# Query blocks outermost, with the rest of the layer run inside the next block's attention

## The chip, the cores and the metric

The kernel runs on one core of one Trainium2 chip. A core has five engines that run side by side and meet only through semaphores: TensorE (PE in the profile; its weight loads are listed as PEld) multiplies matrices, VectorE (DVE) and ScalarE (ACT) work on rows of 128 partitions and can read the accumulators, GpSimd (POOL) works between tiles of SBUF, and SyncE (SP) issues the DMAs of this kernel. Each engine takes its instructions in the order in which they were written. PSUM, where TensorE writes, has 8 banks; one bank holds a tile of 128 x 512 float32.

The metric is the time of one execution on the device, in microseconds (us). Lower is better.

## The reference

One transformer block with adaptive layer norm, on 2048 rows of 512 features, 32 heads of 16 features, a feed-forward width of 1792, all in float32:

```python
mod = (_silu(c) @ w_mod).reshape(c.shape[0], 6, 1, -1)
sa, ca, ga, sb, cb, gb = (mod[:, 0], mod[:, 1], mod[:, 2], mod[:, 3], mod[:, 4], mod[:, 5])
h = _layernorm(x, axis=-1) * (1 + ca) + sa
x = x + ga * _A_ref(h, A_wqkv, A_wo)          # softmax attention, 32 heads, then @ wo
h = _layernorm(x, axis=-1) * (1 + cb) + sb
x = x + gb * _B_ref(h, B_w1, B_b1, B_w2, B_b2)  # gelu(h @ w1 + b1) @ w2 + b2
```

The attention is full: every query meets all 2048 keys, `scores = q . k / 4`, then softmax, then the weighted sum of `v`. The gelu is the tanh approximation.

## The kernel before, in words

**Number format.** TensorE is fed values of a reduced format (`float32r`, FR in the code). To keep accuracy each operand is split into a high part (the value rounded to FR) and a low part (the rest), and a product is made of three matmuls: high x high, low x high, high x low (`mm3`, L288). Splitting costs one copy and one subtraction per tile. For the scores the three products lie in the rows of one contraction: 48 rows (3 x 16 features) for a head, and 50 where two rows carry the negative maximum of the query (its high and low part) against rows of ones, so that a score comes out with the maximum already subtracted.

**Tiling.** Rows are split into 4 query blocks of 512 (`NB`, `TB`), keys into 16 chunks of 128 (`NKC`), heads into 8 groups of 4 (`NG`). A unit `u` is one group with one query block, 32 units in all (`NU`); group is the outer loop: `g, qb = divmod(u, NB)`. A step `s` is one key chunk of one unit; there are 512. The four heads of a group lie in two pairs; the two heads of a pair sit in rows 0 to 63 and rows 64 to 127 of the array (`r0 = (j % 2) * 64`), so two matmuls on opposite row halves can run together.

**Stages, one after the other.**

1. Modulation rows, layer norm, transposes, projections. For each block `b` the loop at L431 projects the first quarter of the keys and queries and all of V; then the loop at L480 projects the other quarters for all blocks, with maxima work put between the matmuls (`fill`). Projected q, k, v go to DRAM and come back in the layout of the scores (`build_k`, `build_q`, `load_v`).
2. Attention, the loop at L729. Each step issues four scores (`exp_step`, L712, matmul L724) with the exponentials on ScalarE (L727), two maxima pairs for a unit further on (`next_max`, `max_pair`, L359: two matmuls at L369 into one tile of two banks, one reduction of 1024 columns per partition on VectorE at L371), and the four `p @ v` matmuls of the step before (`pv_step`, L538, matmul L545). The `v` tiles carry a column of ones, so that the sum of the exponentials comes with the product. `max_rows` (L373) ends a unit's maxima: a reduction, a TensorE transpose, a copy, a split on GpSimd, and three DMAs that bring the row maxima into rows 48 and 49 of the query tile.
3. Output projection of block 0 runs inside the last unit's steps (`hooks`, L694); the others, the second layer norm and the feed-forward follow from L756 on. For each of 4 x 14 chunks of the feed-forward width `load_f` and `split_f` (L568, L576) load and split both weight matrices' tiles, `ffn1` (L760) makes 12 matmuls, one Gelu on ScalarE and a split, and `ffn2` (L777) adds 12 matmuls into four banks that stay open for the block. The list `plan` puts the other blocks' output projection and layer norm at fixed places among the chunks.

**PSUM.** Maxima have two tiles of two banks (`ps_mx`), scores one tile of two banks and one of one bank, used in turn (`ps_e`; three scores are evacuated by one 1024-wide and one 512-wide activation), `p @ v` one bank. Seven banks serve the loop with 4 + 3, one is for `pv`.

**Queues.** The whole order is written out by hand (`tc.manual_schedule()`). All DMAs are issued from SP, in order; one that has to wait for its data holds those behind it. Waits are semaphores set where a tile is written, read or reused.

## Time and profile before

| | |
|---|---|
| median of 3 runs | 2246.9 us (2242.72 to 2248.88) |
| profiled execution, first to last instruction | 2241.2 us |
| mean granted TensorE clock | 0.988 |
| TensorE busy | 1876.3 us, 84% |
| VectorE busy | 1555.4 us, 69% |
| ScalarE busy | 1189.5 us, 53% |
| GpSimd busy | 251.2 us, 11% |
| DMA | 121.87 MB, mean 54 GB/s |

The profiled execution is one run under the hardware profiler; 2241.2 us is its span, and the runs' median lies 5.7 us above that. "Busy" for TensorE is not the same as working at full rate: matmuls are pipelined, the next starts before the last has drained, and the listed duration of one holds that drain. The rate is read from the distance between starts. In a row of the groups view, "x1024 | 1245.7, 1226 | 401.0 <-PE mx L369 398.3" means 1024 instructions, 1245.7 us busy in all, 1226 ns each in the mean, and 401.0 us in which the engine sat idle just before them, of which 398.3 ended when TensorE finished a matmul of line 369. In a row of the timeline the first number is the start in us from the start of the span, the second the length, "x2" the count of instructions merged, and the bracket the idle time before and what ended it. Names left and right of "<-" are the tile written and the tiles read. The clock column is the share of full TensorE clock that the throttle granted.

### The profile page before, as it was taken

The page shows a single profiled execution, that of the slowest core. Times are in us where ns is not written, and L with a number is a line of the kernel's source. Part 1 is how long each engine was busy: PE and PEld are TensorE (multiplying, and loading weights), DVE is VectorE, ACT ScalarE, POOL GpSimd, SP SyncE. Part 2 cuts the span into 40 slices and gives each one's busy share as a digit, 9 for nine tenths or more (in the row PEclk, how much of TensorE's full clock was granted, in tenths as well). Part 3 has the DMA queues.
Part 4 walks back from the last instruction along what each step waited for, and adds up shares of the span by engine and source line. Part 5 has one row for each costly group of instructions (what it writes and reads, how often), then busy time and mean ns, then how long its engine had stood idle before and what let it go on. Part 6 is the DMA issues. An engine that isn't in the chain of part 4 may idle for free.

```text
span 2241.2 us, 27287 instructions
## 1 busy us (share of the span) xinstructions
PE 1876.3 (84%) x10586; PEld 884.1 (39%) x10586; DVE 1555.4 (69%) x1563; ACT 1189.5 (53%) x1597; POOL 251.2 (11%) x250
## 2 busy tenths in 40 slices
PE   8889788787888787878877887888788889999999
PEld 6655322222222222222222222222222235778787
DVE  5245677777777777777777777777777845773653
ACT  2211466666666666666666666666666664221222
POOL 3100001000000000000000000000000102453553
PEclk9998899999999999999999999999999999999999
DMA  6642410030030003000300300030000124432331
GB/s 235 173 168 95 77 26 21 11 60 11 11 51 11 11 11 52 11 11 13 58 11 11 51 11 11 11 51 11 11 15 17 44 82 120 130 113 75 113 113 57
DMA packets 93325, 121.87 MB, mean 54 GB/s; under 512 B 13114, under 2 KB 52026, under 8 KB 91834
## 3 DMA queue, kind: packets, MB, share of 16 engines
q1 hardware_dynamic: 93196, 120.13, 20.4%
q8 instruction: 83, 1.36, 0.3%
q14 instruction: 46, 0.38, 0.1%
HBM read 88.42 MB, written 31.67 MB: 54 GB/s over the span
## 4 chain that ended last, share of the span: by engine, by line
PE 70%; ACT 21%; issue 4%; DVE 3%; POOL 1%; DMA 1%; SPq 0%; ACTq 0%; POOLq 0%; DVEq 0%
PE pv L545 22%; PE e L724 21%; ACT p L727 20%; PE e L294 12%; PE mx L369 6%; PE mx L790 4%; PE e L649 2%; PE pv L790 1%; ACT osb L531 1%; DVE mxp L371 1%; PE mx L724 0%; DVE parts L305 0%; POOL w2l L583 0%; DMA rb<-rden 0%; DVE xin L263 0%
## 5 line engine op out<-in xcount | busy, mean ns | idle before, releaser
L371 DVE TENSOR_REDUCE mxp<-mx 128x2 f32<-128x1024 f32 x1024 | 1245.7, 1226 | 401.0 <-PE mx L369 398.3
L727 ACT ACTIVATE p<-e 128x1024 f32<-128x1024 f32 (+1 forms) x1323 | 1005.7, 809 | 548.5 <-PE e L724 544.1
L724 PE MATMUL e<-qst,kst 50*128 50x512 f32 x1984 | 633.6, 481 | 313.3 <-ACT p L727 306.8
L724 PEld LDWEIGHTS e<-qst,kst 50*128 50x128 f32 x1984 | 249.9, 184 | 939.4 <-ACT p L727 778.7
L545 PE MATMUL pv<-p,vg 128*32 128x512 f32 x4096 | 548.9, 607 | 0.0
L369 PE MATMUL mx<-kst,qst 48*128 48x512 f32 x2048 | 528.5, 417 | 0.0
L369 PEld LDWEIGHTS mx<-kst,qst 48*128 48x128 f32 x2048 | 233.4, 187 | 16.7 <-issue 12.3
L384 POOL CAST m<-mr 16x128 fp32r<-16x128 f32 x32 | 9.0, 280 | 1464.3 <-DVE mr L382 1464.3
L768 ACT ACTIVATE g<-e,b_c 128x512 f32<-128x512 f32 x56 | 38.6, 689 | 248.0 <-PE e L294 248.0
L545 PEld LDWEIGHTS pv<-p,vg 128*32 128x32 f32 x4096 | 80.9, 108 | 188.6 <-issue 183.1
L772 DVE TENSOR_TENSOR glo<-g,ghi 128x512 fp32r<-128x512 f32 x56 | 57.6, 1028 | 105.8 <-ACT ghi L771 105.7
L294 PE MATMUL e<-hThi,w 128*128 128x512 f32 x256 | 76.8, 447 | 22.6 <-DVE parts L305 19.3
L581 POOL TENSOR_TENSOR w1l<-w1r,w1h 128x512 fp32r<-128x512 f32 x56 | 76.8, 1371 | 164.5 <-DVE w1h L580 144.9
L304 ACT ACTIVATE parts<-e 128x512 fp32r<-128x512 f32 x32 | 19.1, 597 | 127.1 <-PE e L294 124.7
L583 POOL TENSOR_TENSOR w2l<-w2r,w2h 128x512 fp32r<-128x512 f32 x56 | 79.4, 1417 | 6.9 <-DVE w2h L582 6.5
L294 PE MATMUL e<-p,w1h 128*128 128x512 f32 x224 | 75.5, 398 | 3.8 <-ACT h L251 2.2
L790 PE MATMUL mx<-w2h,glo 128*128 128x512 f32 x168 | 66.1, 393 | 3.0 <-DVE glo L772 3.0
L294 PEld LDWEIGHTS e<-hThi,w 128*128 128x128 f32 x256 | 52.2, 213 | 40.7 <-DVE parts L305 22.2
L790 PE MATMUL mx<-w2h,ghi 128*128 128x512 f32 x168 | 65.6, 390 | 0.0
L790 PE MATMUL mx<-w2l,ghi 128*128 128x512 f32 x168 | 65.5, 390 | 0.0
L305 DVE TENSOR_TENSOR parts<-e,parts 128x512 fp32r<-128x512 f32 x32 | 21.8, 683 | 44.0 <-ACT parts L304 44.0
L582 DVE CAST w2h<-w2r 128x512 fp32r<-128x512 f32 x56 | 44.4, 792 | 6.9 <-issue 6.6
(129 smaller groups left out, 1254.4 us busy)
## 6 DMA issues: line engine op xcount, KB each, us to landing
qk<-parts SPq DMA_DIRECT2D x32, 512.0 KB
w1r<-in_B_w_dram SPq DMA_DIRECT2D x56, 256.0 KB
w2r<-in_B_w_dram SPq DMA_DIRECT2D x56, 256.0 KB
qst<-qk SPq DMA_DIRECT2D x192, 64.0 KB
kst<-qk SPq DMA_DIRECT2D x42, 256.0 KB
wmod<-in_w_mod_dram SPq DMA_DIRECT2D x6, 1024.0 KB
v<-vst SPq DMA_DIRECT2D x8, 664.0 KB
vg<-v SPq DMA_DIRECT2D x8, 664.0 KB
```

The lines of the kernel that those rows point to most:

```text
L294: te.matmul(ps, p, q, start=i == 0, stop=i == len(terms) - 1)
L369: te.matmul(ps[:, a], q[r0 : r0 + KR, p, qc * P : (qc + 1) * P], k[r0 : r0 + KR, p, kr * TB : (kr + 1) * TB], start=True, stop=True)
L371: ve.tensor_reduce(mxp[u][:, 2 * p : 2 * p + 2, qc, kr], ps, axis=AX.X, op=ALU.max, negate=True)
L545: te.matmul(cur_pv[0][32 * j : 32 * (j + 1)], vg[g][:, kc, j * VW : j * VW + 32], pt.pop(e), start=kc == 0, stop=kc == NKC - 1)
L581: gp.tensor_tensor(alo, a, ahi.bitcast(F32), op=ALU.subtract)
L582: ve.tensor_copy(bhi, b)
L583: gp.tensor_tensor(blo, b, bhi.bitcast(F32), op=ALU.subtract)
L649: te.matmul(ps[0], *terms[i], start=i == 0, stop=i == len(terms) - 1)
L724: te.matmul(ps[:, i] if n == 2 else ps, k[r0 : r0 + KX, p, kc * P : (kc + 1) * P], q[r0 : r0 + KX, p], start=True, stop=True)
L727: ac.activation(pb if n == 2 else pb[:, 0], ps, AF.Exp, scale=SCALE)
L772: ve.tensor_tensor(glo, g, ghi.bitcast(F32), op=ALU.subtract)
L790: te.matmul(acc[qb][t], p[:, sl], q, start=f == 0 and n == 0, stop=f == NF - 1 and n == 2)
```

## The change

The file is largely rewritten. What it does, part by part:

- **Order of units.** `qb, g = divmod(u, NG)`: the query block is now the outer loop, so that block 0 has all its heads after 8 of the 32 units. The keys and values of a group are therefore loaded once per unit (`load_k` in two halves of 1024 keys, five half tiles in turn) and not once per group.
- **The loop.** `CYCLE` is a list of 17 entries, worked through again and again: 12 times `Y`, 3 times `p`, 2 times `b`. A `Y` issues one score of 512 queries x 128 keys for the exponential and one maxima score of 128 queries x 512 keys on the other row half, then the activation (512 wide) and the reduction (512 wide). A `p` is one `pv_step`; a `b` takes the next 4 or 6 matmuls of the background work.
- **Banks.** All 8 banks are single: three in turn for the exponential's scores, three for the maxima, one for `pv`, one for the background.
- **Background.** `block0` holds the projections that are not needed at once; `ffn_block(b)` is a generator with the output projection, the layer norm, the transposes and the feed-forward of block `b`. It runs in the `b` entries of the block after it; what is left after the last score (block 3, above all) runs in the last loop with four banks. Pauses are written as "not before so many `Y`s" (`clock`, `later`).
- **Feed-forward arithmetic.** The Gelu instruction is replaced by its tanh form: an `Identity` with the bias and a `Tanh` on ScalarE, and 7 GpSimd instructions. The second matrix's products are summed in three parts of 5, 5 and 4 chunks, each added to the result in SBUF.
- **Weights.** `wo`, `w1`, `w2` are split once, during the first six units, written to DRAM in split form, and read from there for each block.
- **Maxima rows.** A 32 x 32 block transpose on VectorE takes the place of the TensorE transpose and the copy; 8 DMAs of rows take the place of 2.
- **Start.** 96 of the maxima scores are made before the loop; of the projections only the first half of the keys' groups (2 of 4 quarters), block 0's queries of these, and V are made there.

```diff
-NM = 32
-FILL0 = 3
-AHEAD = 10
+HS = S // 2
+LEAD = 96
+CYCLE = ("Y", "Y", "Y", "p", "Y", "Y", "b", "Y", "Y", "Y", "b", "Y", "Y", "p", "Y", "Y", "p")
+PARTS = ((0, 5), (5, 10), (10, NF))
...
-    def max_pair(u, i):
-
-        g = u // NB
-        q, k = qst[u], kst[g]
...
-        ps = bank_mx()
-        for a in range(2):
-            r0 = a * 64
-            te.matmul(ps[:, a], q[r0 : r0 + KR, p, qc * P : (qc + 1) * P], k[r0 : r0 + KR, p, kr * TB : (kr + 1) * TB],
-                      start=True, stop=True)
-        ve.tensor_reduce(mxp[u][:, 2 * p : 2 * p + 2, qc, kr], ps, axis=AX.X, op=ALU.max, negate=True)
+    def mx_mm():
...
+        a, i = 1 - i % 2, i // 2
+        kr, p, qc = i // 8, (i // 4) % 2, i % 4
...
+        ps = take("mx")
+        r0 = a * 64
+        te.matmul(ps, qst[u][r0 : r0 + KR, p, qc * P : (qc + 1) * P],
+                  kh(u, kr // 2)[r0 : r0 + KR, p, (kr % 2) * TB : (kr % 2 + 1) * TB], start=True, stop=True)
...
+        def red():
+            ve.tensor_reduce(mxp[u][:, hc, kr : kr + 1], ps, axis=AX.X, op=ALU.max, negate=True)
+            if last:
+                max_rows(u)
...
+    def max_rows(u):
+        m = mn[u % 2]
+        ve.tensor_reduce(m[:, :16], mxp.pop(u), axis=AX.X, op=ALU.min)
+        mt = small.tile([P, 32], F32, tag="mt", name="mt")
+        ve.transpose(mt, m)
...
+    ring("e", (0, 1, 2))
+    ring("mx", (3, 4, 5))
+    ring("pv", (6,))
+    ring("bg", (7,))
...
+    def exp_mm():
...
+        ps = take("e")
+        te.matmul(ps, kh(u, kc // 8)[r0 : r0 + KX, p, (kc % 8) * P : (kc % 8 + 1) * P], qst[u][r0 : r0 + KX, p],
+                  start=True, stop=True)
...
+            pt[n] = ppool.tile([P, TB], F32, tag="p", name="p")
+            ac.activation(pt[n], ps, AF.Exp, scale=SCALE)
...
+    def o_prep(b, k):
...
+        def div():
+            ve.reciprocal(dn, dn)
+            sy.dma_start(rden_d[b][k * 8 : (k + 1) * 8].rearrange("h (a f) -> (h a) f", f=32), dn)
...
+            gp.tensor_tensor(ob, ob, rb, op=ALU.mult)
+            gp.tensor_copy(tgt[:, 0], ob)
+            gp.tensor_tensor(tgt[:, 1], ob, tgt[:, 0].bitcast(F32), op=ALU.subtract)
...
+        def ffn1(i):
...
+            def evac(ps):
+                h, s = tmp("h"), tmp("u")
+                ac.activation(h, ps, AF.Identity, scale=0.5, bias=b1_h[:, i : i + 1])
+                gp.tensor_tensor(s, h, h, op=ALU.mult)
+                gp.tensor_scalar(s, s, 4 * 0.044715, 1.0, op0=ALU.mult, op1=ALU.add)
+                gp.tensor_tensor(s, s, h, op=ALU.mult)
+
+                def second():
+                    ac.activation(s, s, AF.Tanh, scale=2 * 0.7978845608028654)
+                    gt[i] = f.tile([P, 2, TB], FR, tag="g", name="g", bufs=6)
+                    gp.tensor_tensor(s, s, h, op=ALU.mult)
+                    gp.tensor_tensor(h, s, h, op=ALU.add)
+                    gp.tensor_copy(gt[i][:, 0], h)
+                    gp.tensor_tensor(gt[i][:, 1], h, gt[i][:, 0].bitcast(F32), op=ALU.subtract)
+
+                later(9, second)
...
+        def ffn2(lo, hi):
...
+            yield lambda: all(i in gt for i in range(lo, hi))
+            for t in range(4):
+                sl = slice(t * P, (t + 1) * P)
+
+                def evac(ps, t=t):
+                    y = tmp("y")
+                    ve.tensor_tensor(y, ps, gb_b, op=ALU.mult)
+                    gp.tensor_tensor(x2[t], x2[t], y, op=ALU.add)
...
+                yield from group("bg", [(gt[i][:, a, sl], wt[2, i][:, w]) for i in range(lo, hi)
+                                        for a, w in ((0, 0), (0, 1), (1, 0))], evac)
...
-    for s in range(NS):
...
-        for j in range(4):
-            exp_step(s, j)
-            if j % 2:
-                new += next_max()
-        if s:
-            pv_step(s - 1)
...
+    while cur["n"] < 4 * NU * NKC:
+        for o in CYCLE:
+            if o == "Y" and cur["n"] < 4 * NU * NKC:
+                if cur["n"] % 4 == 0:
+                    step_start(cur["n"] // 4)
+                a = exp_mm()
+                r = mx_mm() if mi[0] < 64 * NU else None
+                a()
+                if r:
+                    r()
+                advance()
+            elif o == "p":
+                if first:
+                    first = False
+                else:
+                    pv_step()
+            elif o == "b":
+                nb += 1
+                bg(6 if work and len(work) <= NB and nb % 2 else 4)
...
+    ring("bg", (0, 1, 2, 7))
+    while work:
+        for _ in range(3):
+            bg(1)
+        advance()
+        try_prep()
```

`group(bk, terms, evac)` takes a bank of the ring, issues the matmuls of `terms` into it one by one, and calls `evac` behind the last; `bg(n)` advances the background by `n` matmuls, and returns early where a pause or a missing tile holds it. `step_start` issues the loads of the next units' keys, queries and values and the weight splitting.

More of the change, by code (lines that the diff above doesn't have):

```diff
@@ L102, in block_kernel @@
     gp.memset(mhalf, -0.5)
+    mn = [const.tile([P, 32], F32, name=f"mn{i}") for i in range(2)]
+    for t in mn:
+        gp.memset(t, 0.0)
     modc = const.tile([P, 2, KC, 2], F32, name="modc")
@@ L208, in mod_cols @@
     def mod_cols(v, r):
-        ps = bank()
+        ps = take("pr")
         for fc in range(KC):
@@ L331, in heads, with kh @@
+        n = range(KC)
+        yield from group(bk, [(hi[:, i, sl], wv[:, j, i]) for i in n for j in range(2)]
+                         + [(lo[:, i, sl], wv[:, 0, i]) for i in n], evac)
+    qst, mxp = {}, {}
+    def kh(u, h):
+        return khalf[(2 * u + h) % 5]
     def heads(w, g, part, a, t0, t1):
@@ L426, in block_kernel, with mx_pair @@
+    def mx_pair():
+        reds = [mx_mm(), mx_mm()]
+        for f in reds:
+            f()
+    ring("pr", (0, 1, 2, 6, 7))
+    ring("mx", (3, 4, 5))
+    rows = ln1(0)
+    split_w(0, fast=True)
+    warm = bank(3, "warm")
+    for i in range(NWARM):
+        te.matmul(warm[:, :P], ident, ident, start=True, stop=True)
+    psm = take("pr")
+    mod_part(psm, 0)
+    ev = ln1_t(0, rows, lambda: mod_part(psm, 1))
+    mrow = mod_copy(psm)
     mod_cols(0, mrow)
     ev()
-    split_w(4)
-    wms = [load_wm(4, 0), load_wm(3, 1)]
@@ new lines, in block_kernel, with bg @@
+    pools["old"] = [wcm2, scm, wcm, hcm]
+    work = [block0()] + [None] * NB
+    hold = [None]
+    def bg(n):
+        while n > 0 and work:
+            if hold[0]:
+                if not hold[0]():
+                    return
+                hold[0] = None
+            if work[0] is None:
+                b = NB - len(work)
+                work[0] = ffn_block(b)
+            r = next(work[0], None)
+            if r is None:
+                work.pop(0)
+            elif r is MM:
+                n -= 1
+            else:
+                hold[0] = r
```

998 lines of the change are left out of this document (435 added, 563 removed).

## The prediction

> **What bounds the kernel now.** I read the stages first: one view of five stretches of the span (times in us; each engine's busy time, then granted clock, DMA share, GB/s).
>
> ```profile
> span 2241.2 us, 27287 instructions
> ...
> 0.00:121.00 121.00, 103.19 (x488) 78.81 (x489) 46.98 (x99) 33.44 (x54) 26.20 (x37) 0.94 0.65 202
> 121.00:238.50 117.50, 100.91 (x366) 62.44 (x364) 66.47 (x68) 16.26 (x29) 5.80 (x6) 0.90 0.34 121
> 238.50:1811.00 1572.50, 1264.89 (x7881) 438.21 (x7878) 1213.31 (x1053) 1011.42 (x1341) 43.19 (x77) 1.00 0.13 26
> 1811.00:1870.00 59.00, 54.81 (x307) 19.25 (x306) 16.09 (x31) 40.62 (x46) 1.73 (x3) 0.94 0.08 23
> 1870.00:2241.20 371.20, 352.47 (x1554) 285.36 (x1552) 212.55 (x313) 87.81 (x130) 174.31 (x127) 1.00 0.36 109
> ```
>
> The columns are PE, weight load, VectorE (DVE), ScalarE (ACT), GpSimd (POOL). Three regimes follow each other: projections until 238.5, attention until 1870, feed-forward to the end. In 238.5 to 1811 no engine is full: 496 steps (a step is one key chunk of one unit) take 1572.5 us, 3.17 us each, with DVE at 77%, ACT at 64%. In the last 371 us PE is full and ACT and DVE have room. The engines that limit one stage idle in the other.
>
> The groups of instructions, then the timelines, say why attention takes 3.17 us:
>
> ```profile
> L371 DVE TENSOR_REDUCE mxp<-mx 128x2 f32<-128x1024 f32 x1024 | 1245.7, 1226 | 401.0 <-PE mx L369 398.3 <-PE e L724 1.6
> L727 ACT ACTIVATE p<-e 128x1024 f32<-128x1024 f32 x661 | 676.4, 1023 | 450.5 <-PE e L724 447.8 <-PE mx L369 2.8
> L727 ACT ACTIVATE p<-e 128x512 f32<-128x512 f32 x662 | 393.4, 594 | 98.0 <-PE e L724 96.4 <-PE mx L369 1.6
> ```
> ```profile
> 1001.70 0.49 PE L724 MATMUL e<-qst,kst 50*128 50x512 f32 x2 [0.94 <-ACT p L727]
> ...
> 1002.03 0.40 PE L369 MATMUL mx<-kst,qst 48*128 48x512 f32 x2
> 1002.30 1.02 ACT L727 ACTIVATE p<-e 128x1024 f32<-128x1024 f32 x1 [0.16 <-PE e L724]
> ...
> 1002.48 1.23 DVE L371 TENSOR_REDUCE mxp<-mx 128x2 f32<-128x1024 f32 x1 [0.45 <-PE mx L369]
> ...
> 1003.89 2.04 ACT L727 ACTIVATE p<-e 128x512 f32<-128x512 f32 x3 [0.57 <-PE e L724]
> ...
> 1004.15 2.38 DVE L371 TENSOR_REDUCE mxp<-mx 128x2 f32<-128x1024 f32 x2 [0.45 <-PE mx L369]
> ...
> 1004.54 0.50 PE L724 MATMUL e<-qst,kst 50*128 50x512 f32 x1 [0.21 <-ACT p L727]
> ...
> 1004.54 0.73 PE L369 MATMUL mx<-kst,qst 48*128 48x512 f32 x2
> ```
>
> ACT waits for PE's scores, PE waits for ACT to free the bank (0.94 us in the first row), and the maxima queue behind on in-order PE, so DVE waits 0.39 us a reduction (401.0/1024). It is a ring of waits with too few buffers. Two reductions take 2.38 us, not 2x1.226: back to back they overlap by 0.07. ACT's three (594, 1023, 594) take 2.04, an overlap of about 0.06 each. The hand-over from PE costs 0.11 us to ACT (1001.70 + 0.49 to 1002.30) and 0.05 to DVE (1002.03 + 0.40 to 1002.48). The last two rows show an exponential score and a maxima score on opposite row halves starting together.
>
> **The change, part by part.**
>
> *1. One pair per slot, three single banks each.* A slot Y of the new loop issues one exponential score and one maxima score (opposite row halves), one 512-wide activation and one 512-wide reduction; there are 2048 slots, 12 in a cycle, so 170.7 cycles. A cycle also has 3 pv steps and 2 background calls of 4 or 6 matmuls. Prices:
>
> ```profile
> 1005.20 1.06 PE L545 MATMUL pv<-p,vg 128*32 128x512 f32 x8
> 1006.20 0.50 PE L724 MATMUL e<-qst,kst 50*128 50x512 f32 x2
> 1006.53 0.39 PE L369 MATMUL mx<-kst,qst 48*128 48x512 f32 x2
> 1006.77 0.40 PE L724 MATMUL e<-qst,kst 50*128 50x512 f32 x1
> ```
> ```profile
> L376 DVE TENSOR_REDUCE mn<-mxp 128x16 f32<-128x64 f32 x32 | 7.0, 220 | 1.1
> L795 DVE TENSOR_TENSOR y<-mx,gb_b 128x512 f32<-128x512 f32 x12 | 7.6, 681 | 3.4 <-PE mx L790 3.4
> L651 DVE TENSOR_TENSOR x2a<-e,x2a 128x512 f32<-128x512 f32 x12 | 8.3, 691 | 40.4 <-PE e L649 40.4
> L225 DVE BATCH_NORM_STATS2 bst<-x2a 128x6 f32<-128x512 f32 x12 | 8.0, 670 | 0.0
> L768 ACT ACTIVATE g<-e,b_c 128x512 f32<-128x512 f32 x56 | 38.6, 689 | 248.0 <-PE e L294 248.0
> L768 ACT ACT_TABLE_LOAD x1 | 1.3, 1283 | 0.0
> ```
> ```profile
> 2148.00:2204.00 56.00, 56.00 (x249) 46.25 (x248) 29.09 (x34) 13.91 (x21) 32.97 (x25) 1.00 0.39 118
> ```
>
> No row has a 512-wide reduction of scores. Through 1226 at 1024 and 220 at 64 runs 153 + 1.048n, that is 0.69 us at 512; 512-wide reads of PSUM cost 0.68 and 0.69. Bounds: 0.61 (half of 1226) and 1.226. I take 0.69, less 0.07 of overlap: 0.622 a slot, 7.46 a cycle, 7.54 with the per-unit minimum and transpose (taken as 2x0.22, every 64 slots). ACT: 12x0.533 = 6.4. PE: a pair 0.23 (1006.77-1006.53), a pv step 0.45, and about 0.1 for each change of tile form (8 pv to the next score 1.00; the first pair after it 0.33); a full-array matmul 0.226 (249 in 56.00 us). 12x0.226 + 3x0.45 + 10x0.226 + 10 changes x0.1 = 7.3. So DVE leads, PE is close behind.
>
> *2. Background work inside attention.* Cover is DVE's backlog. With three banks, when a pair issues DVE holds three reductions, 1.87 us. PE is back after 0.23 + 0.1 + 0.226k + 0.1, and a score needs another 0.50 + 0.05. For k = 4 that is 1.88, nothing lost; for 6, 2.33, 0.47 lost. A pv step (0.45) is covered. When a 12-matmul group ends inside a call, the next group waits for the one bank 7: 0.39 + 0.69 (ACT) + 0.11 and 0.05 of hand-over - 0.23 = 1.0 us; by sizes 6, 4, three of five ends fall inside, 0.5 us a cycle. First feed-forward layer: 7.54 + 0.47 + 0.5 = 8.5. Second: DVE evacuates (0.67 groups x 0.62 = 0.41) behind its backlog, dry about 1.3 us in half the cycles, else 0.47: 8.85. Output projection: 0.83 x (0.62 + 0.67 + 0.18) and ends: 9.2. By matmuls (168, 168, 56 a block) 8.8.
>
> In slots: remaining projections are 264 matmuls at 8 a cycle, 33 cycles at 7.6 = 251. A block has 392 at 10 a cycle, 39 cycles, plus some 45 slots of written-in pauses; block 0 starts near slot 555, block 1 near 1082, block 2 near 1612, whose last 66 matmuls run past slot 2048. That gives 111 full cycles x 8.8 = 977, and 27 with nothing in the background x 7.54 = 204. The pv bank waits for its copy-out once a unit (0.6 us of ACT, mostly covered): 32 x 0.4 = 13; I add 20 for waits I can't place. Loop: 1465.
>
> *3. Feed-forward elementwise work goes to GpSimd.* Gelu becomes 7 GpSimd operations a chunk round one Tanh.
>
> ```profile
> L562 POOL TENSOR_TENSOR wo_lo<-wo_raw,wo_hi 128x512 fp32r<-128x512 f32 x4 | 5.1, 1268 | 48.0 <-DVE wo_hi L561 48.0
> L384 POOL CAST m<-mr 16x128 fp32r<-16x128 f32 x32 | 9.0, 280 | 1464.3 <-DVE mr L382 1464.3
> L190 POOL COPY sel_b<-sel 128x256 f32<-128x256 f32 x1 | 0.4, 397 | 1.2 <-DVE sel L189 1.2
> ...
> L583 POOL TENSOR_TENSOR w2l<-w2r,w2h x56: 1279/1290/1752, 1884.7 to 2218.3; 128x512 fp32r<-128x512 f32 x56
> ```
>
> Two-input operations: 1.28. One-input, 512 wide: 280 at 128 and 397 at 256 give 0.63 (bounds 0.40 and 1.28). 5x1.28 + 2x0.63 = 7.7 us a chunk. In the loop PE brings a chunk every 12/10 x 8.6 = 10.3 us, so it hides; the Tanh stands 9 slots (6.5 us) behind its evacuation and needs 0.7 + 3.2 us first, so ACT does not wait. Weight splitting once instead of four times takes 112 DVE and 112 GpSimd operations from the end and puts 32 tiles into the first six units, where GpSimd is free.
>
> *4. DMA and SP.* Keys are reloaded per unit (12 issues, 1.5 MB), split weights read per block, maxima rows by 8 issues.
>
> ```profile
> 1870.72 0.32 SPq L533 DMA_DIRECT2D o<-osb  x1
> ...
> SPq L390 <- DMA m<-m: 36.3, 32, 2.0
> ```
>
> Some 40 issues a unit at 0.32 us are 13 of 46 us; a landing was waited for 2.0 us at most (last row: total, times, longest), and loads have 8 steps (20 us) of lead. A store waiting for GpSimd holds the loads behind it by some 5 us. Taken as zero; bounds 0 and 32 x 2 = 64 us.
>
> *5. Start.* Before the loop stand 10 query/key groups and the 16 of V (before: 32 and 16), with 96 single maxima among them.
>
> ```profile
> L304 ACT ACTIVATE parts<-e x8: 597/597/598, 25.1 to 104.5; 128x512 fp32r<-128x512 f32 x8
> ...
> L319 ACT ACTIVATE vst<-e x16: 595/600/613, 34.6 to 118.1; 128x512 f32<-128x512 f32 x16
> ```
>
> The last V tile left at 118.1. Up to there it has 3 groups fewer (36x0.23 = 8 us) and 24 pairs of maxima more (24 x (0.23 + 0.1) = 8): 118 again. Then 5 groups, each with 8 maxima at 0.622 = 5 us, and 8 maxima more: 30 us. Loop begins at 148 where 238.5 stood.
>
> *6. End.* After the last slot block 3 has everything before it: three pv steps 1.4, copy-out 0.6, four DMA trips at 2.0, then 3.2 on GpSimd, 13 us; output projection 48x0.226 = 11; normalisation and transposes with 4 x (1.28 + 1.91) on GpSimd, about 18 (an estimate from these rows); then 14 chunks x 7.7 = 107 on GpSimd with 8 additions (10); last 39 matmuls at half clock, additions, store: 19. Sum 178, against 371.
>
> Sum: 148 + 1465 + 178 = 1791 us of span. The run median, 2246.9, lies 5.7 above the profiled span; so 1797.
>
> **The rivals.**
>
> *A, GpSimd binds* (or ACT reloads its table at each Tanh; no row shows a Tanh beside Exp, the one reload seen took 1.28 us, 112 of them 143 us). If its operations take 1.75 (the maximum above), a chunk is 12.3 > 10.3: 42 chunks x 2 in the loop, 14 x 4.6 at the end: 1797 + 148 = 1945. For it: that maximum. Against: it stands where DVE works on SBUF; here DVE reads PSUM.
>
> *B, the waits stay:* the pairing doesn't speed the ring and a step costs 3.17 as before, with the background in its idle 23%: 512 x 3.17 = 1623, total 1955; with the background on top (111 x 1.26) 2095. Against: the rows at 1004.54.
>
> *C, better:* background stalls hidden, 7.8 a cycle: 1331 + 33, total 1696.
>
> *D, slower than before: PE falls to half clock in the loop.*
>
> ```profile
> 163.60:249.00 85.40, 72.94 (x256) 42.22 (x254) 49.24 (x51) 14.79 (x23) 0.73 (x2) 0.82 0.34 102
> 249.00:1811.00 1562.00, 1255.57 (x7838) 434.70 (x7838) 1205.91 (x1047) 1004.97 (x1333) 43.19 (x77) 1.00 0.13 25
> ...
> 165.81 2.81 PE L294 MATMUL e<-hThi,w 128*128 128x512 f32 x8 [1.91 <-DVE parts L305]
> ```
>
> Where projections and maxima mixed, with waits of 1.9 us, the clock averaged 0.82: 36% of the time at half. A cycle at half clock is 2x7.3 = 14.6. With share h the mean is 1/((1-h)/8.8 + h/14.6); it passes the break-even cycle (2241-148-178)/170.7 = 11.2 at h = 0.54. At 36% the total is 2080, still faster; at 70%, 2440. Against: attention had 0.94 us waits all along and stayed at 1.00, and the new loop leaves PE idle less. The Trainium skill ("TensorE: Matmul & The Clock Gate", section on a second failure mode, cycling through PSUM banks) says that small pauses between groups while banks rotate make the gate oscillate between half and full clock. By that rule the loop, which rotates three banks, would go the way of D; the trace so far speaks against it, since attention rotated banks with waits at 1.00.
>
> **How the numbers follow.** My forecast (1710 to 1880, the stall estimates and a 20% error of the end) 0.60; A 0.14; B 0.10; C 0.09; D beyond break-even 0.05; 0.02 elsewhere. Low 1690 takes in C, high 1940 takes in most of A; beyond lie B and D. Faster by over 0.3% (what this kernel's runs can tell from no change) 0.94, same 0.01, slower 0.05.
>
> **What would show it.** First exponential near 148 us. Reductions of 0.69 us, nearly back to back between background calls; DVE at 85 to 90% in the loop. Start of e and mx rows together, clock 1.00. Gaps on DVE ended by PE after groups ending within a call. Loop end near 1613, then some 178 us with GpSimd full. Wrong if ACT waits for GpSimd before Tanh, if table loads appear beside Tanh, if 512-wide reductions cost far from 0.69, or if PE's clock drops in the loop.

## The result, and the profile after

| | before | after |
|---|---|---|
| median of 4 runs each, same chip | 2247.9 us (2242.7 to 2267.4) | 2227.7 us (2220.7 to 2230.8) |
| ratio, 95% interval | | 0.990 (0.986 to 0.994) |
| span of the profiled execution | 2241.2 us | 2225.6 us |
| granted TensorE clock | 0.988 | 0.917 |

Run times here and below are medians of a kernel's fast runs; three runs of later kernels, over 1.5% above the fastest run of the same kernel, are left out.

Faster by 1%, where 20% was forecast. The forecast of 1797 us is 431 us short, and 2228 lies far above its range. By the forecast's own stages: start 171 for 148 (+23), loop 1842 for 1465 (+377), end 213 for 178 (+35); the run stands 2 us above its span for 6 (-4).

The page of the profile after, its first rows, the clock row, and the chain that ended last by engine:

```profile
span 2225.6 us, 29467 instructions
...
PE 1925.6 (87%) x10544; PEld 855.4 (38%) x10544; DVE 1412.5 (63%) x2317; ACT 1235.2 (56%) x2302; POOL 751.7 (34%) x787
...
PEclk8998969999789999999989999999899999996777
...
PE 67%; DMA 10%; POOL 8%; DVE 6%; ACT 4%; issue 3%; SPq 2%; POOLq 0%; DVEq 0%; ACTq 0%
```

Two thirds of the chain is TensorE, 6% VectorE: the loop was to be VectorE's. The stages, in the same columns as in the prediction, with two units of the loop under them (a unit is 64 slots):

```profile
0.00:171.00 171.00, 140.20 (x590) 88.56 (x590) 92.38 (x174) 44.58 (x70) 47.65 (x69) 0.90 0.59 175
171.00:2013.00 1842.00, 1661.30 (x9540) 678.51 (x9541) 1299.79 (x2111) 1169.96 (x2202) 567.30 (x590) 0.94 0.42 104
2013.00:2225.00 212.00, 124.05 (x416) 88.30 (x414) 20.30 (x32) 20.68 (x32) 136.75 (x128) 0.72 0.27 96
...
476.00:524.00 48.00, 48.00 (x302) 19.36 (x296) 40.76 (x66) 35.87 (x68) 7.90 (x10) 1.00 0.47 109
1342.00:1396.00 54.00, 51.02 (x312) 20.67 (x306) 41.43 (x67) 37.09 (x70) 19.43 (x20) 1.00 0.41 115
```

In the loop VectorE is busy 71% (85 to 90% forecast) and TensorE 90%. The last two rows stand at full clock: TensorE fills 48 of 48 us with projections in the background and 51 of 54 with the feed-forward. The costliest groups (busy, mean ns | idle before, releaser):

```profile
L380 DVE TENSOR_REDUCE mxp<-mx 128x1 f32<-128x512 f32 x2048 | 1298.8, 685 | 449.4 <-PE mx L375 388.4
L539 ACT ACTIVATE p<-e 128x512 f32<-128x512 f32 x2048 | 1092.7, 599 | 611.4 <-PE mx L375 399.9
...
L562 PE MATMUL pv<-p,vg 128*32 128x512 f32 x4096 | 577.0, 637 | 6.2 <-ACT osb L548 6.2
```

The reduction took the 0.69 us that was forecast. VectorE and ScalarE both wait for TensorE's scores. The third row holds the mistake: 4096 records for 512 value steps are 8 a step, although the code issues 4, one for each head. The operands are plain float32, and the trace lists each such matmul twice; the float32r ones of the scores (x2048 for 2048) are listed once. One cycle of the new loop at full clock, from TensorE's timeline:

```profile
1341.20 0.50 PE L533 MATMUL e<-qst,kh 50*128 50x512 f32 x1
...
1341.85 1.07 PE L562 MATMUL pv<-p,vg 128*32 128x512 f32 x8
1342.85 0.49 PE L533 MATMUL e<-qst,kh 50*128 50x512 f32 x1
...
1344.50 0.50 PE L533 MATMUL e<-qst,kh 50*128 50x512 f32 x1
...
1345.39 1.06 PE L562 MATMUL pv<-p,vg 128*32 128x512 f32 x8
...
1347.06 1.66 PE L283 MATMUL bg<-w,g 128*128 128x512 f32 x6
1348.65 0.50 PE L533 MATMUL e<-qst,kh 50*128 50x512 f32 x1
...
1349.57 1.20 PE L283 MATMUL bg<-w,g 128*128 128x512 f32 x4
1350.70 0.49 PE L533 MATMUL e<-qst,kh 50*128 50x512 f32 x1
```

From score to score the cycle takes 1350.70 - 1341.20 = 9.50 us, and TensorE has no gap in it. A value step with the change of form behind it takes 1.00, a background call of 6 takes 1.59 and one of 4 takes 1.13. The forecast's sum for TensorE was 7.3. With 0.9 a value step, as the same row read rightly gives, it is 8.65; the remaining 0.85 makes a change of form 0.18 in the mean and not 0.1.

Waits that the forecast had at nothing, or within the 20 us that it could not place, from the list of waits (total, times, longest):

```profile
POOL ob L599 <- DMA rb<-rden: 205.3, 11, 48.5
ACT p L539 <- PE pv L562: 140.6, 163, 6.1
DVE dn L595 <- DMA dn<-ou: 102.5, 11, 26.2
ACT wqk L163 <- DMA wraw<-in_A_wqkv_dram: 34.9, 4, 21.8
```

and what one of them does, from the timeline of all engines:

```profile
581.85 0.35 DVE L595 RECIPROCAL dn<-dn 128x32 f32<-128x32 f32 x1 [15.58 <-DMA dn<-ou]
...
582.80 0.79 PE L375 MATMUL mx<-kh,qst 48*128 48x512 f32 x1 [14.91 <-DVE mxp L380]
...
586.21 1.57 ACT L539 ACTIVATE p<-e 128x512 f32<-128x512 f32 x3 [17.34 <-PE mx L375]
```

The reciprocal of the softmax sums stands in VectorE's order before its operand has landed. VectorE stops for 15.6 us with the reductions behind it, then TensorE stops, then ScalarE for 17.3: the loop's rings empty, and the clock stands at 0.50 from 571.6 to 588.6 us.

### The profile page after: what moved, and what is told of

Same layout as the page of the kernel before. It is cut to its first block, busy times and chain, and to the rows that moved or that the text cites. A ratio compares the mean times of both kernels' runs of the same rounds, so it can differ in the third digit from the quotient of the medians.

```text
span 2225.6 us, 29467 instructions
## 1 busy us (share of the span) xinstructions
PE 1925.6 (87%) x10544; PEld 855.4 (38%) x10544; DVE 1412.5 (63%) x2317; ACT 1235.2 (56%) x2302; POOL 751.7 (34%) x787
## 4 chain that ended last, share of the span: by engine, by line
PE 67%; DMA 10%; POOL 8%; DVE 6%; ACT 4%; issue 3%; SPq 2%; POOLq 0%; DVEq 0%; ACTq 0%
PE pv L562 20%; PE bg L283 19%; PE e L533 18%; PE mx L375 8%; DVE mxp L380 3%; PE pr L283 2%; DMA wf<-in_B_w_dram 2%; DMA w<-w1s 2%; ACT p L539 1%; DMA dn<-ou 1%; DMA wraw<-in_A_wqkv_dram 1%; DVE y L712 1%; DMA rden<-dn 1%; POOL h L692 1%; ACT h L683 1%
## 5 line engine op out<-in xcount | busy, mean ns | idle before, releaser
L380 DVE TENSOR_REDUCE mxp<-mx 128x1 f32<-128x512 f32 x2048 | 1298.8, 685 | 449.4 <-PE mx L375 388.4
L539 ACT ACTIVATE p<-e 128x512 f32<-128x512 f32 x2048 | 1092.7, 599 | 611.4 <-PE mx L375 399.9
L375 PE MATMUL mx<-kh,qst 48*128 48x512 f32 x2048 | 742.3, 459 | 51.1 <-DVE mxp L380 45.9
L533 PE MATMUL e<-qst,kh 50*128 50x512 f32 x2048 | 733.5, 453 | 15.4 <-ACT p L539 14.4
L533 PEld LDWEIGHTS e<-qst,kh 50*128 50x128 f32 x2048 | 329.8, 192 | 616.3 <-ACT p L539 465.1
L375 PEld LDWEIGHTS mx<-kh,qst 48*128 48x128 f32 x2048 | 326.3, 192 | 88.6 <-DVE mxp L380 76.0
L283 PE MATMUL bg<-w,g 128*128 128x512 f32 x672 | 212.3, 443 | 89.1 <-POOL g L693 47.9
L283 PE MATMUL bg<-pc,w 128*128 128x512 f32 x672 | 193.8, 420 | 26.3 <-ACT h L683 16.3
L283 PEld LDWEIGHTS bg<-w,g 128*128 128x128 f32 x672 | 124.4, 201 | 168.8 <-POOL g L693 53.3
L691 POOL TENSOR_TENSOR u<-u,h 128x512 f32<-128x512 f32 x56 | 71.8, 1283 | 136.7 <-ACT u L689 136.7
L686 POOL TENSOR_TENSOR u<-u,h 128x512 f32<-128x512 f32 x56 | 71.7, 1281 | 4.7
```

The source lines that it names most:

```text
L283: te.matmul(ps, p, q, start=i == 0, stop=i == len(terms) - 1)
L375: te.matmul(ps, qst[u][r0 : r0 + KR, p, qc * P : (qc + 1) * P], kh(u, kr // 2)[r0 : r0 + KR, p, (kr % 2) * TB : (kr % 2 + 1) * TB], start= ...
L380: ve.tensor_reduce(mxp[u][:, hc, kr : kr + 1], ps, axis=AX.X, op=ALU.max, negate=True)
L533: te.matmul(ps, kh(u, kc // 8)[r0 : r0 + KX, p, (kc % 8) * P : (kc % 8 + 1) * P], qst[u][r0 : r0 + KX, p], start=True, stop=True)
L539: ac.activation(pt[n], ps, AF.Exp, scale=SCALE)
L686: gp.tensor_tensor(s, s, h, op=ALU.mult)
```

## The experiments

Ratios are against the kernel before, run on the same chip. bfloat16 probabilities and values, where used, give up accuracy in the value products only.

### Is it the value step? Single-pass value products in both kernels

```diff
-        vg[u] = vgpool.tile([P, NKC, VG], F32, tag="vg", name="vg")
+        vg[u] = vgpool.tile([P, NKC, VG], BF, tag="vg", name="vg")
-            pt[n] = ppool.tile([P, TB], F32, tag="p", name="p")
+            pt[n] = ppool.tile([P, TB], BF, tag="p", name="p")
```

Changed kernel:

> The changed kernel with p and v kept in bfloat16, so that the product p @ v, now 8 matmuls a step, becomes 4 (it loses accuracy in that product). Theory 1 (TensorE is the bound of the loop, because a pv step costs two passes, 0.9 us, where the prediction counted 0.45): 512 steps x 0.45 = 230 us less TensorE work, VectorE becomes the bound, 2228 falls to about 2000 us (1960 to 2060). Theory 2 (the loop loses its time to waits behind DMA round trips and single-bank copy-outs, and to the half clock after them): the waits stay, 2150 us or more.

Kernel before, same edit:

> The kernel before with the same edit (p and v in bfloat16, p @ v in 4 matmuls a step; loses accuracy there). If the ring of waits between TensorE and ScalarE binds the old loop and pv fills its idle time, nothing changes: 2247 us. If pv stands in that ring, as in the chain that ended last (pv 22% of the span), up to 512 x 0.45 = 230 us go: about 2030 to 2100 us. Either way it says whether the price of pv alone decides between the two kernels.

The changed kernel took 2191.4 us (ratio 0.971, 0.965 to 0.977), at a clock of 0.78: by the number the second theory, 2150 us or more. The one before became slower, which neither expectation had: 2407.1 us (1.068, 1.064 to 1.072), at 0.62. In the changed kernel's groups, timeline and windows:

```profile
L563 PE MATMUL pv<-p,vg 128*32 128x512 bf16 x2048 | 242.2, 463 | 4.4 <-ACT osb L549 4.3
```
```profile
1366.38 0.40 PE L563 MATMUL pv<-p,vg 128*32 128x512 bf16 x4
1366.71 0.50 PE L534 MATMUL e<-qst,kh 50*128 50x512 f32 x1
```
```profile
1360.00:1407.00 47.00, 44.42 (x242) 24.29 (x241) 39.62 (x67) 36.44 (x71) 20.96 (x21) 1.00 0.43 91
585.40:630.20 44.80, 44.73 (x190) 24.39 (x188) 39.71 (x67) 34.98 (x66) 0.46 (x2) 0.50 0.34 57
```

The records halve, but the price falls to a third: a value step with the change of form behind it takes 0.33 us (1366.38 to 1366.71) where it took 1.00, and the forecast's price was 0.55 (0.45 and 0.1). With it TensorE's sum is 9.50 - 3x0.67 = 7.5 a cycle, close to the 7.3 that was assumed, because the cheaper step makes up for the dearer changes of form. The first window is nearly one unit (64 slots in 47.2 us) at full clock with feed-forward in the background: 8.9 us a cycle, where the forecast had 8.8. So with TensorE's sum near what was assumed, the cycle comes out as assumed. But the second window, without background, runs at half clock throughout, and in the whole loop the time at half clock rises from 219 to 797 us. The price was the error of the cycle; most of what its removal gains goes with the clock, and 36 us are left.

### What does the clock follow? Redundant work in the kernel before

Two kernels built on the slow one (the kernel before with bfloat16 value products), both with redundant work: every maxima matmul issued twice, or every value matmul four times.

> The kernel before with p and v in bfloat16, which alone ran its attention at half clock and took 2407 us, and with every maxima matmul issued twice into the same place, so that TensorE again does about the work of the kernel before (two pairs more for one pv pass less). If activity sets the clock, the clock comes back to 1.00 and the time to about 2250 us (2200 to 2300). If bfloat16 itself lowered the clock, it stays at 0.62 and the time rises above 2407.

> The kernel before with p and v in bfloat16 and every pv matmul issued four times into the same sum (numerator and denominator both grow fourfold, so the quotient stays), so that pv again holds TensorE about as long as the two float32 passes did. Theory 'the clock follows how much of the array pv keeps at work': clock 1.00 in attention again and about 2250 us. Theory 'bfloat16 itself, or anything but the float32 passes, leaves the clock low': clock 0.6 and 2500 us or more.

The first took 2631.4 us (1.170, 1.167 to 1.174), the second 2241.7 (0.996, 0.994 to 0.998): with more work than the bfloat16 kernel it is 165 us faster. The same 600 us of attention in the three, single value products first, then maxima twice, then value products four times:

```profile
400.00:1000.00 600.00, 539.29 (x2047) 233.02 (x2047) 418.77 (x360) 353.92 (x464) 9.74 (x22) 0.50 0.11 20
```
```profile
400.00:1000.00 600.00, 582.12 (x2428) 307.77 (x2426) 374.64 (x324) 320.15 (x412) 12.33 (x24) 0.50 0.08 16
```
```profile
400.00:1000.00 600.00, 482.26 (x4545) 203.29 (x4547) 464.51 (x403) 388.79 (x516) 11.19 (x26) 1.00 0.12 22
```

TensorE is busy 97% of the second row at half clock and 80% of the third at full clock. So the busy time of the profile doesn't set the clock, and the number format of the value products alone doesn't either (all three are bfloat16); by these rows, matmuls that use 48 or 50 rows of the array count for little, and the value products, which use all 128 rows and in groups of four all columns, for much. The Trainium skill ("TensorE: Matmul & The Clock Gate", Part 1) says that the gate goes by how busy TensorE has recently been; by that, the second row would be the one at full clock. These rows disagree if busy is read from the profile; if it is work in the array they fit, though no run here counts that work.

The third kernel also prices the float32 step. In its timeline a value step has 16 bfloat16 matmuls:

```profile
1002.21 1.05 PE L545 MATMUL pv<-p,vg 128*32 128x512 bf16 x16
1003.19 0.50 PE L726 MATMUL e<-qst,kst 50*128 50x512 f32 x2
```

It holds TensorE for 0.98 us, the float32 step with its 4 matmuls, listed as 8, for 1.00: a float32 matmul is listed twice and costs here as much as four bfloat16 ones.

### The stalls and the end

The reciprocal put 24 slots behind the issue of its load, and GpSimd's products 16 slots behind theirs and not 8; and the last block's Gelu and additions in their old form (Gelu on ScalarE, subtraction and additions on VectorE), one edit in each kernel:

```diff
-            later(12, lambda: ready.append((qb, g // 2)))
+            later(12, lambda: o_den(qb, g // 2))     # load dn
+        def inv():                                    # reciprocal, store
+            ...
+        later(24, inv)
...
-        later(8, div)
+        later(16, div)
```
```diff
+                ac.activation(h, ps, AF.Gelu_apprx_tanh, bias=b1_c[:, i : i + 1])
+                ac.activation(gt[i][:, 0], h, AF.Copy)
+                ve.tensor_tensor(gt[i][:, 1], h, gt[i][:, 0].bitcast(F32), op=ALU.subtract)
```

> The changed kernel with the softmax denominators fetched and inverted 24 slots after their DMA, apart from the rest of the output projection's preparation, and GpSimd's products 16 slots after their loads: VectorE no longer stands before a landing. Theory 1: only the stalls themselves go, 8.5 + 15.6 + 11.1 us inside the loop and part of 26 at its end: 40 to 60 us less, about 2175 us. Theory 2: each stall also starts half-clock windows and delays the background, 80 to 120 us less, about 2130 us.

> The changed kernel with block 3's feed-forward (the part after the last score) done as in the kernel before: Gelu and the high part on ScalarE, the low part, the additions and the layer norm's copies on VectorE. If GpSimd binds the end (98 us busy of its last 125), the 213 us after the last score become about 135 (392 matmuls x 0.226 = 89 plus the hand-overs): 2150 us. If DMA round trips and the order of the groups bind it, 20 us or less go.

The late reciprocal gave 2183.4 us (0.968, 0.964 to 0.973), 44 less; VectorE's wait for the landing of the sums falls from 102.5 us to 5.0, and the time at half clock in the loop falls from 219 to 165 us. The old end gave 2154.1 us (0.956, 0.951 to 0.961), 74 less. Its stages, loop and end:

```profile
171.00:2013.00 1842.00, 1654.67 (x9528) 675.69 (x9532) 1298.98 (x2111) 1170.65 (x2202) 569.62 (x591) 0.94 0.42 105
2013.00:2149.00 136.00, 103.22 (x434) 80.47 (x426) 42.91 (x70) 23.51 (x34) 6.71 (x6) 0.86 0.43 149
```

The loop is the same to the microsecond and the end falls from 212 to 136. GpSimd bound it, one Gelu chunk after the other, as the timeline of the changed kernel shows:

```profile
2093.11 1.04 POOL L684 TENSOR_TENSOR u<-h 128x512 f32<-128x512 f32 x1
...
2100.74 1.04 POOL L684 TENSOR_TENSOR u<-h 128x512 f32<-128x512 f32 x1
```

7.63 us a chunk, 7.7 forecast. What the forecast missed in the end is its head, as the timeline of the changed kernel has it: GpSimd's normalisation waits 25.7 us for the row sums' trip through DRAM and the rest of the output projection 18.7 for GpSimd; 34 us pass before it runs, where 13 were counted.

All three mends in one: both above, and the projection weights of the last two quarters, for which ScalarE stood 21.8 us (the row of `wqk` above), loaded before the loop:

> The changed kernel with three edits together: denominators inverted late and GpSimd's products after their loads; the raw tiles of the last two weight quarters loaded ahead into tiles of their own, so that ScalarE no longer stands 10 and 22 us before their landing; block 3's feed-forward on ScalarE and VectorE as in the kernel before. If the waits are separate costs they add: 2228 less about 50 (late), 30 (weights) and 75 (end): about 2070 us. If the stalls feed each other through the half clock, less than 2040; if one hides behind another, 2110 or more.

2094.5 us (0.931, 0.928 to 0.934): 133 less than the changed kernel. The early loads were not run alone. If the three add, they are worth 133 - 44 - 74 = 15, a remainder no larger than its uncertainty, since it is taken between chips on which the kernel before took 2257 and 2248 us. It is less than ScalarE's wait: GpSimd's part of the same split then waits, and TensorE for it 16.6 us.

### Do the parts add, and can the clock be bought back?

The mended kernel with bfloat16 value products, and that with identity products, read by nobody, in background calls that had nothing else to do:

> The same three edits with p and v in bfloat16 (loses accuracy in p @ v). In the units of the bfloat16 run that had no half clock a cycle took 8.9 us against 10.1 in the changed kernel. If pv's price were all, 170 cycles x 1.2 = 200 us less than the run with three edits: about 1870. If the clock is granted by how much TensorE does, the lighter loop falls to half clock more often and gives most of it back: 2000 to 2060 us, mean clock below 0.85.

> As the run before, and wherever the background is held by a written pause the slot's background call issues as many 128x128 matmuls of the identity into the background's bank, which nothing reads: TensorE does more, for nothing. If activity sets the clock, the clock in units 6 to 8 and at the changes of block rises to full and the time falls by 30 to 100 us against the run without them; if the half clock has another cause, the time is the same or longer by the added work (some 27 cycles x 10 x 0.22 = 60 us of TensorE, mostly in its idle time).

2017.5 us (0.899, 0.893 to 0.904) at a clock of 0.83, and 2046.3 (0.906, 0.899 to 0.912), with ranges that overlap. A stretch that has an empty background for the most part, without and with the filler:

```profile
476.00:618.00 142.00, 140.55 (x646) 75.02 (x645) 126.12 (x210) 110.76 (x209) 18.41 (x23) 0.65 0.52 127
```
```profile
476.00:618.00 142.00, 139.47 (x862) 85.89 (x858) 122.98 (x206) 107.12 (x206) 16.58 (x21) 0.96 0.51 123
```

The filler brings the clock back there, but VectorE finishes 206 operations for 210 in the same time: what the faster clock gives is spent on the filler. A clock below full is not by itself a loss. The 29 us between the two kernels lie elsewhere and are not explained.

### Banks

Two banks for the exponential's scores instead of three, and two for the background:

```diff
-    ring("e", (0, 1, 2))
+    ring("e", (0, 1))
-    ring("bg", (7,))
+    ring("bg", (2, 7))
```

> The run with three edits (2094.5 us), with two banks for the background and two instead of three for the exponential's scores. Theory 'TensorE is the bound of the loop and the copy-outs of the one background bank stop it' (34.7 us of gaps ended by VectorE's y, 20.9 by ScalarE's h, 10 by pf in the loop): 40 to 60 us less, about 2045. Theory 'the exponential needs its third bank as much': same or slower, 2095 to 2130.

2330.6 us (1.031, 1.024 to 1.038): 236 slower than its base and more than either theory had. TensorE's queue now waits for ScalarE at 1188 of 2048 exponential scores (663 in its base, 462.5 us):

```profile
PEld e L539 <- ACT p L545: 868.2, 1188, 1.4
...
PE e L539 <- ACT p L545: 210.3, 532, 1.0
```

The third score bank is a part of the change that pays; the waits at the single background bank, priced at 0.5 us a cycle, are the cheaper side. The two edits were not run apart.

### Weight splitting

In the first units the feed-forward's weight tiles were split two steps after the issue of their load; here it is four:

> The run with three edits (2094.5 us), with the splitting of the stored weights four steps after their loads instead of two. GpSimd stood 8 to 14 us at a time before those landings in the first six units, and ScalarE and TensorE behind it (units 1 and 2 took 70 us where others took 51). If these are that wait, units 1 and 2 fall to about 53 us: 30 us less, 2060. If the first units are slow from their DMA load or from the projections' own hand-overs, the same within 10 us.

2044.7 us (0.908, 0.904 to 0.911), 50 less than its base. Units 1 and 2 take 49 and 57 us for 70 each, and GpSimd's wait for those loads falls from 141.3 us to 45.2: in its order it had stood before tiles that had not landed, with the maxima's and the projections' splits behind it.

### The order of the cycle

The forecast was still far off, so the order of value steps (p), background calls (b) and pairs (Y) was tried, first with the value steps as far apart as possible:

```diff
-CYCLE: YYY p YY b YYY b YY p YY p
+CYCLE: YYY p YY b YY p YY b YY p Y
```

> Changed kernel with its cycle written in another order: the third group of value products moved so that no more than four pairs stand between two of them (YYY p YY b YY p YY b YY p Y for YYY p YY b YYY b YY p YY p). Work and instruction counts are unchanged. Theory 1, that the stretches of seven pairs without a value product let the granted clock fall and that ScalarE's waits for the buffers that the value products free cost part of the loop: ScalarE's waits on PE at the exponential fall by more than half, the stretches at half clock (about 219 us of the loop) get shorter, and the time falls from 2228 to about 2150 to 2190. Theory 2, that in float32 TensorE is simply full (streams of 1661 us in a loop of 1842) and the order only moves the gaps about: within 15 us of 2228. Theory 3, that products placed earlier meet tiles of exponentials that are not ready: slower, 2250 or more.

> The same order of the cycle in the version with all four edits (late reciprocal, early loads of the feed-forward weights, old form of the end, late splitting of the weights), 2044.7 us. Theory 1: ScalarE's wait for the value products at the exponential (147 us there) goes, TensorE's gaps in the loop (about 100 us) fall by half, and the time is 1990 to 2020. Theory 2 (TensorE full): 2030 to 2060. Theory 3: above 2070.

> The version before it with probabilities and values in bfloat16 (which gives up accuracy in the value products): a value step is 4 matmuls for 8. The version without late splitting and in the old order took 2017.5 at a clock of 0.83. Late splitting alone should give about 1970. Theory 1 (the gaps between value products set the clock): the clock rises above 0.87 and the time is 1880 to 1940. Theory 2 (what counts is how much array work there is in a cycle, not where it stands): the clock stays near 0.83 and the time is 1950 to 1985.

All three were slower than their bases: 2302.2 us (1.025, 1.023 to 1.027), against 2227.7; 2102.5 (0.936, 0.934 to 0.938), against 2044.7 (the mended kernel, whose early loads are the projection's, as above, and not the feed-forward's); and 2020.2 (0.899, 0.895 to 0.904), whose partner follows below. In the mended kernel the clock rose from 0.954 to 0.969 and ScalarE's wait for value products (147.5 us) went, as theory 1 had it, but its wait for maxima scores rose from 313.7 us to 497.0, and the kernel was slower: theory 3 by the number, and for a reason that it didn't give. TensorE's timeline in the mended kernel of that order shows why:

```profile
432.76 0.50 PE L539 MATMUL e<-qst,kh 50*128 50x512 f32 x1
...
433.11 0.61 PE L539 MATMUL e<-qst,kh 50*128 50x512 f32 x2
...
434.04 0.50 PE L539 MATMUL e<-qst,kh 50*128 50x512 f32 x1 [0.31 <-ACT p L545]
...
434.51 1.07 PE L568 MATMUL pv<-p,vg 128*32 128x512 f32 x8
```

Over the seam of the cycle four pairs follow each other, and the fourth waits for a bank (three banks, and ScalarE needs about 0.6 us for each). Four pairs take 434.51 - 432.76 = 1.75 us. In the cycle shown above the pairs in groups of 3 and 2 take 0.89 (1344.50 to 1345.39) and 0.65 (1341.20 to 1341.85): the third pair costs some 0.24, the first two 0.33 each. So 3, 2, 3, 2, 2 costs 2x0.89 + 3x0.65 = 3.73 us and 4, 2, 2, 2, 2 costs 4.35, 0.62 us a cycle or 106 in the loop. If that is so, a spread order that keeps the groups of three must win:

```diff
-CYCLE: YYY p YY b YYY b YY p YY p
+CYCLE: YYY p YY b YYY p YY b YY p
```

> The mended version once more with only its cycle reordered: value products and background calls alternate (YYY p YY b YYY p YY b YY p), with the same groups of 3, 2, 3, 2, 2 pairs as the old order, where the order tried before made a run of four pairs over its seam. Theory 1, that the run of four was what cost (four scores of 0.33 us each against a ring of three banks that ScalarE empties at 0.6 us): TensorE's gaps ended by the exponential (44 us in the order before, 3 us in the old one) stay under 10 us, ScalarE's wait for the value products (147 us in the old order) goes, the clock stays at 0.96 or more, and the time is 2000 to 2040, below the old order's 2044.7. Theory 2, that a value product at every second group costs more wherever it stands: 2080 to 2110 again. Theory 3, that TensorE is full and the order is worth nothing: 2040 to 2055.

> The mended version in the old order with probabilities and values in bfloat16 (accuracy in the value products is given up), as the partner of the next run. Late splitting was worth 50 us in float32: about 1970 at a clock near 0.83.

> The same in bfloat16 with the alternating order. If the distance between two value products sets the clock: clock above 0.87 and 1900 to 1945. If the amount of array work in a cycle sets it: clock as in its partner and within 15 us of it.

In float32: 1999.4 us (0.889, 0.885 to 0.893), 45 less than the old order and 103 less than the run of four. The loops of the three, old order, run of four, alternating:

```profile
166.00:1904.00 1738.00, 1637.31 (x9522) 670.22 (x9521) 1300.47 (x2113) 1169.78 (x2199) 558.34 (x582) 0.96 0.45 111
```
```profile
165.00:1953.00 1788.00, 1660.90 (x9521) 675.82 (x9519) 1301.26 (x2113) 1172.93 (x2199) 558.27 (x581) 0.98 0.43 108
```
```profile
164.00:1858.00 1694.00, 1601.59 (x9518) 659.90 (x9520) 1298.45 (x2112) 1167.26 (x2199) 559.38 (x582) 0.98 0.46 114
```

The second and third have the same clock and differ by 94 us, close to the 106 worked out. The first and third differ by 44: the time at half clock falls from 126 to 61 us, worth at most 33, and TensorE's gaps by 9. In a unit at full clock nothing is gained (unit 5: 48.8 us in both). So by these figures the alternating order wins mainly by the clock, not by ScalarE's wait. With single-pass value products the same order gains nothing: 1977.7 us (0.879, 0.874 to 0.885) in the old order at 0.846, 1992.0 (0.886, 0.880 to 0.892) in the alternating one at 0.837, with ranges that overlap. That is the number expected if the amount of array work in a cycle sets the clock, and not where it stands.

The version in full accuracy with the alternating order, 1999 us, is 10% faster than the changed kernel and 11% faster than the one before.

## Why the prediction was wrong

- **Start** (148, took 171): 23 us over. Not tested; its row shows a clock of 0.90 and TensorE idle 31 of 171 us, which the sum had at nothing.
- **The pair and the reduction** (step 1): right. 685 ns for 0.69, and a third pair of a group 0.24 for 0.23; the second pair of a group, 0.33, is counted with the changes of form. The ring of waits is gone, as step 1 said: TensorE stands idle 15.4 us in all before the exponential's scores.
- **The value step** (step 1, "a pv step 0.45"): the step that failed. The row it came from said x8 in 1.06 us, and that is one step and not two. A row of before had it, not used: 4096 records for 512 steps.

```profile
L545 PE MATMUL pv<-p,vg 128*32 128x512 f32 x4096 | 548.9, 607 | 0.0
```

  With it, and 0.18 for a change of form in place of 0.1, TensorE needs 9.5 us a cycle and not 7.3, and passes VectorE's 7.54. Of the 2.2 us that the sum lacked, the value step is 3x0.45 = 1.35 and the changes of form 0.85. "DVE leads, PE is close behind" is the wrong way round.
- **Background stalls** (step 2): priced for a loop in which VectorE's backlog is the cover. It has next to none, since TensorE has no gap, so each background matmul counts whole. 8.8 a cycle became 9.9 to 10.9, 10.26 in the mean (52.9 to 57.9 us per unit, in the nine units at full clock), 7.6 with projections 9.1, 7.54 without background 8.9 (in a unit with 10 of its 48 us at half clock): 111x1.46 + 33x1.5 + 27x1.4 = 249 of the loop's 377.
- **In-order waits** (steps 2 and 4, DMA "taken as zero; bounds 0 and 64 us", "20 for waits I can't place"): wrong in size and place. Late reciprocal 44, early loads 15 (a remainder, as above), late splitting 50: 109 us by the runs, the clock that falls behind each stall included. With the 249 of the cycles that is 358 of the 377; the rest is not placed. The bound came from the waits of an order in which the loads had long landed.
- **GpSimd** (step 3): right, 7.63 a chunk for 7.7, and hidden in the loop: of the 47.9 us that TensorE waits for its chunks, 47.0 lie behind the loop. The trace has one table load, at the start, and none beside Tanh. Rival A falls. B and C have no term for a dearer TensorE either.
- **End** (step 6, 178, took 213): GpSimd bound it, as said; the chain through DRAM before it took 34 us and not 13.
- **Rival D, half clock:** partly true, and not for the reason given. 219 us of the loop stand at half clock, at most 110 us of time, mostly behind stalls and around an empty background. That "the new loop leaves PE idle less" was no protection, since the clock stood at 0.50 in a row with TensorE busy 97%; the rotation of banks is not the cause by itself, because units 5 and 20 rotate three banks at 1.00. The share at half clock was 12%, far from the 54% at which D would have ended slower. (By D's own formula a share of 70% gives about 2410 us and not 2440; nothing hangs on it.)

So the direction held because the end (371 to 213 us) and the start (238 to 171) gave 225 us, and the loop took back most: 1842 against 1632 for attention before. The 15 us that are left are what remains of two large terms; that the sign came out as forecast was close to luck.

## What to carry to other kernels

Before a row becomes a price, divide its count by the number of steps in the loop; a float32 matmul can be two records, and four times a bfloat16 one in price. When engines are near each other, price the second one as carefully as the first, since a small error there changes which one binds. And in a merged stream every instruction that may wait for a landing is a stall of the whole loop: put it later than the landing, then look at the groups between changes of form.

## What was not expected of the hardware

- TensorE's clock stood at 0.50 for 600 us in which TensorE was busy 97%, and at 1.00 in one where it was busy 80%. Value products on all 128 rows make the difference: 2241.7 us with each issued four times, 2407.1 with each issued once, at 0.50 as well.
- A float32 matmul is listed as two records and costs as much as four bfloat16 ones: a value step with the change of form behind it takes 1.00 us in float32, 0.33 in bfloat16, and 0.98 with each bfloat16 matmul issued four times.
- A change of tile form costs about 0.18 us in the mean here (9.50 us cycle, ten changes), counted against pairs of 0.226 us; part of it shows in the pairs behind it, of which the first two take 0.33 us each and the third 0.24. The Trainium skill ("TensorEngine Tiling (Array Packing)", Key Properties) says that a change of tiling mode drains TensorE, without a figure; the trace agrees in that each change costs time, and shows no more of what it consists.
- Why the clock falls in one stretch without background and not in the next stays open: in the alternating version unit 7 has 14 us at half clock, units 6 and 8 have none.
